# Two channels per filter matmul, product planes instead of finished sums, and a new order of all queues, in a state-space convolution kernel

## The chip, the cores and the metric

The kernel runs on one core of a Trainium2 chip. A core has five instruction queues that run side by side: TensorE (PE, matmuls), VectorE (DVE), ScalarE (ACT), GpSimd (POOL) and SyncE (SP, which issues DMAs here). The metric is the device time of one execution in microseconds; lower is better. The time before is the median of three runs, 216.46 us (214.34 to 217.51).

## The reference

The input u (2048 positions, 512 channels) is normalized; the normalized xn goes two ways. One is a long convolution per channel, whose filter K is built from 128 complex modes; the other is a small gated network on the single position with the largest router score. The result is `x + s * silu(b)`.

```python
P = jnp.exp(logdA[:, :, None] * l[None, None, :])
K = jnp.einsum("dn,dnl,dn->dl", Cc, P, dB).real
...
Yf = Uf * Kf[None, :, :, :]
y = ...irfft2(Yf...)[:, :, 0, :L]
y = y.transpose(0, 2, 1) + u * Dskip
...
g = _silu(_B_ref(xn, B_w_r, B_w_gate, B_w_up, B_w_down))
return x + s * g
```

The positions l are cast to bf16 first, so only 640 different positions occur: K needs 640 values per channel.

## The kernel before

**Filter values.** A filter position is split into a row (32 of them: multiples of 64, some with 1, 2 or 3 added) and a step (26 of them). For each channel, `GG` holds the 128 modes' values at the 32 rows (real and imaginary) and `QQ` those at the 26 steps. One matmul per channel and part (modes are the 128 partitions, 32 rows the weights, 26 steps the moving columns) adds real and imaginary part in PSUM and gives the channel's 32 x 26 filter values. Channels are worked in four quarters of 128: (0,0), (0,1), (1,0), (1,1); the first figure is the half.

**Rows.** `kgen_g` (L1007) starts each quarter from one row (`WW`) and doubles: rows times a complex multiplier `MB[k]` give further rows. `cmul` (L982) does such a product on VectorE in four instructions: two products into scratch `TT` (`TT<-GG,MB`), then two sums or differences from scratch (`GG<-TT`). Seven of them give 1, 2, 4, 4, 8, 4 and 8 rows.

**Steps.** `exps` (L928) and `sines` (L972) make the magnitudes `E` and the phases in `QQ` on ScalarE, 16 instructions of 512 elements each, both halves at once; `turn` (L995) rotates the start row; `kgen_q` (L1020) joins them on VectorE and gets nine more steps by one complex product (`TT<-QQ,MB`, `QQ<-TT`). The chain between them (`SL`, `MB`) squares the multipliers up.

**From filter to spectrum.** `kgen_mm` (L1033) runs the 256 matmuls of a quarter into two PSUM banks and copies them out as `KE`; `kgen_kx` (L1049) moves values to the order of the index table (24 selection matmuls per quarter with 0/1 matrices, copies `KS`, then `KX`). `ROWS` (L318) and `_kpoints` are that index table; the inline table `c_fd` (tile `FD`) is built from it. `spec` (L1125) multiplies `KX` with `FD` (8 groups of 20 matmuls per quarter), copies each group out as `KF` (a ring of seven), and multiplies it into the input's spectrum `UU`. `inv_a` transforms back (copies `C`), `fin` (L1157) ends the inverse, multiplies with the gate `G` and stores.

**The input's way.** Statistics (`ST`, `LST`), normalized `XN`, moved to `XZN` by DMA, two transform stages (`AU`, `UST`), out to DRAM (`scr_u`) and back as `UU`. The router transposes `XN` through `XT`; the network's weights stream through the ring `WRING`.

**Order.** The order of each queue is written out as a list of operation numbers (`ORDER`, L373); an operation waits by semaphore for those that it depends on, also for earlier ones of its own engine. Copies out of PSUM and some small steps can stand in ScalarE's or VectorE's list; the list decides which engine does them. Buffers share memory: `XR` and `G0` lie over `GG`, `UU0` over `XN`, `UU1` over the first half of `QQ`, `F2U` and one `UST` over its second half, `FD` over `AU` and `WRING`. A function asked for by `activation` that lies in another table than the last one costs an `ACT_TABLE_LOAD`.

Of the kernel before, what the change touches and what calls it, by code (L numbers as in the profile page):

```python
# [7 lines left out]
ACT = mybir.ActivationFunctionType  # L8
# [309 lines left out]
ROWS = [64 * r for r in range(16)] + [64 * r + 1 for r in range(4)] + [64 * r + 2 for r in range(8)] + [64 * r + 3 for r in range(4)]  # L318
# [3 lines left out]
def _kpoints():  # L322


    seq = [[], []]
    for par in range(2):
        for jp in range(8):
            seq[par] += [b + 4 * STEPS[2 * jp + par] for b in ROWS]
        for jp in range(4):
            seq[par] += [1024 + b + 8 * (2 * jp + par) for b in ROWS[:16]]  # L330
    return seq[0][:256] + seq[1][:256] + seq[0][256:] + seq[1][256:]


def tables():
# [29 lines left out]
    for q in range(2):  # L364
# [6 lines left out]

ORDER = dict(
    sync="""  # L373
        9-10 12 11 1 6 3 18 7 4 207 211 13 209 205 17 14-15 203 16 145 92 94 93 90 95 91 96-97 146 141 137 140 139 144 138 143 142 150 149 152 151
        147-148 303-304 213 215 217 219 221 309 223 225 427 314 229 231 227 233 319 241 324 243 428 245 247 249 329 545-547 334 251 253 255 257 259
        429 339 261 344 430 548 550 549 644 646-647 268 648-649 645 748 747 746 744 743 745 788 787 785 789 786 790 828 827 832 830 829 831 847
        849-850 855 857-858 848 866 863 874 872 865 864 856 871 873 884 881 883 882 900 898 897 890 916 908 905 907 925-926 906""",
    scalar="""
        5 0 2 8 19-20 35 34 33 28 25-26 23-24 21-22 29 32 30 44 361 360 362 356 358 86-87 89 359 348 354 159 353 355 350 352 347 357 131 133 135 46
        48 363 50 365-367 406 415 364 375 177 399 409 374 398 272 379 274 380 372 381 419 280 407 282 284 386 391 387 288 417 290 393 392 425 294  # L380
        400 296 298 401 300 302 390 412-414 410 420 408 416 421 306 308 311 313 411 418 517 460 316 349 346 351 345 264 321 323 328 326 239 333 331
        616 471 478 476 336 338 480 484 341 343 486 552 531 558 528 564 561 570 533 567 537 535 573 541 539 543 576-577 579-580 654 583 582 651
        585-586 660 657 666 663 672 627 669 630 634 632 679 636 678 676 675 684 681 753 750 759 765 762 729 726 771 731 768 735 775 774 778 833 836
        834-835 804 807 844 810 813 852 783 860 816-817 819 868 823 822 826 878 894 886 910 899 902 891 914 913 920 889 892 915 924 923""",
    vector="""
        202 54 53 62 61 51 57 59 65 56 52 64 104 58 60 66 55 105 63 100 67 103 68 79 154 69 111 70 108 71 101 72 99 73 109 74 107 75 102 76 98 77
        113 78 106 80 112 81 110 88 114 82 115 84 116 85 117 126 83 118 31 119 36 120 37 121 38 122 39 123 27 124 40 125 156 127 42 128 41 132 129
        134 136 130 162 165 168 171 369 174 371 368 370 179 376-377 180 402 181 378 373 276 183 278 383 185 382 423 186 385 187 388 188 286 190 389
        384 394 192 422 193 292 194 395 195 426 424 397 488 197 431 198 461 433 432 396 435 434 518 437 436 403 439 438 441 440 201 442-444 449 445
        447 446 448 451 450 453 452 457 455 454 462 318 456 464 458-459 519 463 520 466 465 265 618 467-468 489-490 266 237 491-492 617 493-494  # L390
        235-236 495-496 238 521 497-498 474 500 499 240 717 501-502 506 504 587 503 620 505 619 508 507 510 509 514 511-512 482 513 716 516 515 487
        523 522 715 524-525 588-589 719 591 590 718 592-593 553 595 594 555 597 596 556 598 559 263 599 267 605 600-601 562 565 603 571 602 568 604
        574 607 606 609 608 613 610-611 269 612 544 614-615 686 622 621 655 623-624 688 687 652 689-690 661 692 691 667 694 693 664 696 695 673 698
        697 658 699-700 704 701-702 670 703 705-708 640 710 709 638 711-712 642 714 713 643 720-721 754 722-723 751 756 760 757 766 685 682 763 733
        772 739 769 737 741-742 777 792-793 795-796 798 838 799 801 840 802 842 839 841 780 805 808 845 781 811 814 853 784 846 854 861 820 862
        869-870 825 879-880 895-896 887 911 888 912 903-904 921-922""",
    gpsimd="""
        404-405 199 270""",
    tensor="""
# [5 lines left out]
        867 821 824 875-877 893 885 909 901 917-919""",  # L405
# [7 lines left out]
def build(nc, A_u, A_A_re, A_A_im, A_B_re, A_B_im, A_C_re, A_C_im, A_log_dt, A_Dskip,  # L413
# [10 lines left out]
    for k in range(4):  # L424
        tri[k, k:] = 1.0
        mk[k, k] = 1.0

    perm = np.zeros((128, 128))
    for p in range(128):
        g_ = 2 * (p // 16 % 2) + p // 64  # L430
        perm[p, 64 * (p // 32 % 2) + 32 * (p // 8 % 2) + 8 * (p % 8 // 2) + 2 * g_ + p % 2] = 1.0
    sel = np.zeros((128, 64))
    for gp in range(4):
        for k in range(16):
            sel[32 * gp + k, 16 * gp + k] = 1.0
    cb_list = [("PRM", perm), ("SEL", sel), ("F1", T["F1"]), ("FA1", T["FA1"]), ("FA2", T["FA2"]), ("IDB", np.eye(128)), ("E127", e127), ("TRI", tri)]
# [30 lines left out]
    with g.ctx:  # L467
# [6 lines left out]
        UPD = g.buf("UPD", o, [512], BF16)  # L474
        GX = g.buf("GX", o + 1024, [64], BF16)
        K2R = g.buf("K2R", o + 2048, [512], BF16)
        X4 = g.buf("X4", o + 3072, [512], BF16)
        DSK0 = g.buf("DSK0", o + 4096, [256], BF16)
        o += 4096 + 512
# [24 lines left out]
        RH = RT + 9 * KB  # L504
        assert RH + 13 * KB + 256 <= 229344 - SBASE, RH + 13 * KB + 256 - 229344 + SBASE

# [39 lines left out]
        KF = [g.buf(f"KF{i}", RH + 1024 * i if i < 4 else RD + 2560 if i == 4 else RH + 10752 + 1024 * (i - 5), [4, 128], BF16) for i in range(7)]  # L546
# [10 lines left out]
        XT = [g.buf(f"XT{i}", RT + 2048 * i, [2, 4, 128], BF16) for i in range(3)]  # L557
        TB = [g.buf(f"TB{i}", RT + 2048 * i, [1024], BF16) for i in range(4)]
        KE = g.buf("KE", RH + 4096, [8, 8, 26], BF16)
        KS = g.buf("KS", RH + 7424, [4, 320], BF16)  # L560
        DSK = [DSK0, g.buf("DSK1", RH + 9984, [256], BF16)]
        WR4 = g.buf("WR4", RH + 10496, [128], BF16)
        WRC = g.buf("WRC", RH + 12800, [4], BF16)
# [141 lines left out]
        for h, p0 in ((0, 32), (0, 96), (1, 32), (1, 96)):  # L705
            load(DSK[h](DSK[h].a.reshape(2, 2, 64), p0, 1), _dma_rows(A_Dskip, 128 * h, [[64, 2], [256, 2], [1, 64]]), 512)
# [68 lines left out]
        for i in range(4):  # L775
            store(sb(X4, i, 1, 0, [[64, 8], [1, 64]]), XN(XN.a[:, :, i].reshape(8, 64), 0, 1), 1024, w=[X4(None, i, 1)])

# [194 lines left out]
        def sines():  # L972
            memset(PO, qboth(0, 0), 1.0)
            memset(PO, qboth(1, 0), 0.0)
            for k in [8] + list(range(1, 8)):
                act(qboth(0, k), TH(), ACT.Sin, scale=float(4 * k), bias=pi2, table="silu", tokr=["set"])
                act(qboth(1, k), TH(), ACT.Sin, scale=float(4 * k), table="silu", tokr=["set"])

        def scratch(n, w):
            return TT.a[0:4 * n * w].reshape(2, 2, n, w)  # L980

        def cmul(dst_r, dst_i, src, mr, mi, n, w, conj):  # L982

            t = scratch(n, w)
            tt(DV, TT(t[0]), src, MB(bc(mr, (2, n, w))), ALU.mult)
# [47 lines left out]
        def kgen_mm(h, s):  # L1033
            q = Q[h]
            for u in range(4 * s, 4 * s + 4):
# [10 lines left out]
                if u % 2:  # L1046
                    evac(KE(KE.a[u - 1:u + 1].reshape(-1)), bank(bank.a[0:416]))

# [218 lines left out]
```

## Time and profile before

| | |
|---|---|
| median of 3 runs | 216.46 us |
| the profiled execution | 217.09 us |
| its span, first to last instruction | 215.3 us |
| mean granted TensorE clock | 0.937 |
| DMA moved | 38.85 MB |

Busy shares are averages over stages with different limits: normalization and router, then the filter's modes with the input's transform beside them, then four rounds of matmuls, spectrum and inverse, then the output. Lines of a view name the tile written and the tiles read (`GG<-TT`), the shape of one instruction, the count, the busy time in us and the mean in ns, and after the second bar the idle time just before them with what ended it. L585 is the helper for all two-input vector operations, L613 and L614 are one copy helper on ScalarE and on VectorE, L580 is the activation helper, and L650 all matmuls, so groups are told apart by their tiles.

### The profile page before, as it was taken

The page shows a single profiled execution, that of the slowest core. Times are in us where ns is not written, and L with a number is a line of the kernel's source. Part 1 is how long each engine was busy: PE and PEld are TensorE (multiplying, and loading weights), DVE is VectorE, ACT ScalarE, POOL GpSimd, SP SyncE. Part 2 cuts the span into 40 slices and gives each one's busy share as a digit, 9 for nine tenths or more (in the row PEclk, how much of TensorE's full clock was granted, in tenths as well). Part 3 has the DMA queues.
Part 4 walks back from the last instruction along what each step waited for, and adds up shares of the span by engine and source line. Part 5 has one row for each costly group of instructions (what it writes and reads, how often), then busy time and mean ns, then how long its engine had stood idle before and what let it go on. Part 6 is the DMA issues. An engine that isn't in the chain of part 4 may idle for free.

```text
span 215.3 us, 6844 instructions
## 1 busy us (share of the span) xinstructions
PE 155.0 (72%) x2979; PEld 130.0 (60%) x2979; DVE 186.1 (86%) x385; ACT 145.2 (67%) x230; POOL 4.6 (2%) x8
## 2 busy tenths in 40 slices
PE   0043977998487159859886897698799799977560
PEld 0033866876354037636785786698699789876430
DVE  1999999899999889999997699679999457989692
ACT  2579999999999456653133589534971249989961
POOL 2000000001100000000000020000000000000000
PEclk9999999999999999985998899799999889999955
DMA  6940959600678969999599802920059299971457
GB/s 223 376 172 32 160 116 223 259 3 0 203 288 212 364 207 299 329 279 334 141 365 237 209 7 54 292 53 6 0 157 228 47 377 268 182 122 33 100 111 149
DMA packets 37181, 38.85 MB, mean 180 GB/s; under 512 B 10816, under 2 KB 29728, under 8 KB 36640
## 3 DMA queue, kind: packets, MB, share of 16 engines
q1 hardware_dynamic: 34704, 37.53, 62.4%
q10 hardware_dynamic: 2384, 0.90, 1.7%
q8 instruction: 23, 0.38, 0.8%
q14 instruction: 6, 0.05, 0.1%
q0 software_dynamic: 64, 0.00, 0.0%
HBM read 27.92 MB, written 8.39 MB: 169 GB/s over the span
## 4 chain that ended last, share of the span: by engine, by line
ACT 37%; PE 33%; DVE 14%; DMA 9%; issue 4%; SPq 2%; ACTq 0%
PE PB L650 33%; ACT C L621 12%; DMA scr_u<-UST 5%; DVE ST L743 4%; ACT AU L613 4%; ACT G L580 3%; DVE TT L585 3%; ACT UST L613 3%; ACT QQ L580 3%; ACT E L580 2%; SPq L667 2%; DMA XZN<-XN 2%; ACT XN L766 2%; ACT TB L580 2%; DMA X<-in_A_u_dram 2%
## 5 line engine op out<-in xcount | busy, mean ns | idle before, releaser
L650 PE MATMUL PB<-KX,FD 128*128 128x128 bf16 x640 | 45.2, 235 | 6.1 <-ACT KF L613 4.2
L650 PEld LDWEIGHTS PB<-KX,FD 128*128 128x128 bf16 x640 | 41.4, 107 | 8.8 <-ACT KF L613 4.7
L585 DVE TENSOR_TENSOR TT<-GG,MB 128x1024 bf16<-128x1024 bf16 (+3 forms) x56 | 39.3, 741 | 0.1
L613 ACT ACTIVATE KF<-PB 128x512 bf16<-128x512 f32 x26 | 15.4, 599 | 29.0 <-PE PB L650 22.7
L621 ACT ACTIVATE C<-PB 64x512 bf16<-64x512 f32 x48 | 28.3, 590 | 3.7 <-PE PB L650 2.8
L585 DVE TENSOR_TENSOR UU<-UU,KF 128x1024 bf16<-128x1024 bf16 x32 | 21.5, 685 | 6.7 <-ACT KF L613 6.6
L650 PE MATMUL PB<-QQ,GG 128*32 128x26 bf16 x1024 | 21.4, 233 | 3.5 <-issue 2.6
L650 PEld LDWEIGHTS PB<-QQ,GG 128*32 128x32 bf16 x1024 | 19.9, 173 | 5.6 <-issue 3.6
L650 PE MATMUL PB<-AU,F2U 64*128 64x256 bf16 x128 | 14.6, 380 | 11.9 <-ACT UST L613 8.2
L585 DVE TENSOR_TENSOR GG<-TT 128x512 bf16<-128x512 bf16 (+3 forms) x56 | 22.9, 445 | 0.1
L613 ACT ACTIVATE UST<-PB 128x1024 bf16<-128x1024 f32 x15 | 14.9, 1027 | 10.0 <-DMA scr_u<-UST 6.4
L650 PE MATMUL PB<-CB,UU 128*128 128x128 bf16 x256 | 19.2, 229 | 3.1 <-ACT C L621 2.0
L650 PEld LDWEIGHTS PB<-CB,UU 128*128 128x128 bf16 x256 | 17.3, 150 | 4.7 <-ACT C L621 2.9
L650 PE MATMUL PB<-CB,XZN 32*128 32x64 bf16 x256 | 16.2, 343 | 2.3 <-DMA XZN<-XN 0.8
L650 PEld LDWEIGHTS PB<-AU,F2U 64*128 64x128 bf16 x128 | 7.2, 123 | 15.6 <-ACT UST L613 9.6
L650 PEld LDWEIGHTS PB<-CB,XZN 32*128 32x128 bf16 x256 | 13.4, 200 | 4.8 <-ACT AU L613 2.2
L743 DVE BATCH_NORM_STATS2 ST<-X 128x6 f32<-128x512 bf16 x16 | 10.3, 676 | 3.8 <-DMA X<-in_A_u_dram 3.8
L650 PE MATMUL PB<-CB,XN 128*64 128x128 bf16 x128 | 8.3, 314 | 6.4 <-DVE XN L767 5.2
L613 ACT ACTIVATE AU<-PB 128x1024 bf16<-128x1024 f32 x12 | 12.1, 1028 | 0.1
L585 DVE TENSOR_TENSOR QQ<-QQ,E 128x896 bf16<-128x896 bf16 (+1 forms) x12 | 10.3, 865 | 1.9 <-ACT E L580 1.0
L626 DVE CAST C<-PB 64x512 bf16<-64x512 f32 x16 | 11.0, 689 | 0.8 <-PE PB L650 0.5
L650 PEld LDWEIGHTS PB<-CB,XN 128*64 128x64 bf16 x128 | 6.6, 169 | 7.4 <-DVE XN L767 5.5
(122 smaller groups left out, 241.1 us busy)
## 6 DMA issues: line engine op xcount, KB each, us to landing
FD<-c_fd SPq DMA_DIRECT2D x4, 1280.0 KB, 6.0
scr_u<-UST SPq DMA_DIRECT2D x8, 512.0 KB, 7.2
UU<-scr_u SPq DMA_DIRECT2D x8, 512.0 KB, 7.9
UU<-scr_u SPq DMA_DIRECT2D x16, 256.0 KB, 8.3
X<-in_A_u_dram SPq DMA_DIRECT2D x4, 512.0 KB, 6.2
XZN<-XN SPq DMA_DIRECT2D x16, 128.0 KB, 3.8
scr_g<-XN SPq DMA_DIRECT2D x4, 512.0 KB, 6.4
G<-scr_g SPq DMA_DIRECT2D x1, 2048.0 KB, 8.9
```

What stands on the lines that cost most here:

```text
L580: g.op(AC, lambda e: e.activation(out=out.ap, in_=in_.ap, func=func, **kw), w=[out], r=r, cost=cost(AC, out, 0.834) - (43 if in_.buf.space ...
L585: g.op(eng, lambda e: e.tensor_tensor(out=out.ap, in0=a.ap, in1=b.ap, op=op), w=[out], r=[a, b], cost=cost(eng, out, rate))
L613: g.op(AC, lambda e: e.activation(out=out.ap, in_=in_.ap, func=ACT.Copy), w=[out], r=[in_], cost=cost(AC, out, 0.834) - 43, alt=(DV, lambd ...
L621: ins = e.activation(out=o_.ap, in_=i_.ap, func=ACT.Copy)
L626: ins = e.tensor_copy(out=o_.ap, in_=i_.ap)
L650: ins = e.matmul(o_.ap, lhsT=l_.ap, rhs=r_.ap, start=st, stop=sp, **kw)
L667: fn = lambda e: e.dma_start(dst, src)
L743: g.op(DV, lambda e, b=b: e.bn_stats(ST6(ST6.a[b]).ap, X0(X0.a[b]).ap), w=[ST6(ST6.a[b])], r=[X0(X0.a[b])], cost=620)
L766: flex(ov, [iv, mv_, nv, rv], lambda e, ov=ov, iv=iv, nv=nv, rv=rv: e.activation(out=ov.ap, in_=iv.ap, func=ACT.Identity, bias=nv.ap, scal ...
```

## The change

- **Rows.** Doubling stops at 12 rows (1 + 1 + 2 + 4 + 4, planes 20 to 31 of `GG`). The last two row products (12 rows times `MB[6]`, 8 rows times `MB[3]`) fill planes 0 to 19. In the second half (`PROD` false) they are finished by sums as before, in one step each. In the first half (`PROD` true) the four product planes stay: re times re and im times re in `GG`, im times minus im (`NM`) and re times im in a new tile `GP`; the matmuls add them up, four per channel pair where the second half has two.
- **Matmuls.** Two channels lie in one matmul: 64 weight columns (40 for `GP`), 52 moving columns; two column groups of 64 instead of four of 32. 1024 matmuls become 512 + 256. `KE` is copied out four times a quarter instead of twice, and the selection matmuls go from 24 of full width to 48 of half width a quarter.
- **Complex products** write the first product into the destination and add in place.
- **Halves.** `exps`, `sines` and `turn` run per half: 32 + 32 instructions of 256 elements instead of 16 + 16 of 512. `DSK1` is loaded later.
- **Memory.** `TT` halves, `GP` and `NM` are new, `KF` is a ring of five, `XT` lies over the second half of `QQ`, `X4` goes into `K2R`.
- **Index table and order.** `ROWS` is re-ordered to follow the planes (and with it `c_fd` and the selection matrices); all five lists of `ORDER` are new, with other choices of engine for the copies.

```diff
-ROWS = [64 * r for r in range(16)] + [64 * r + 1 for r in range(4)] + [64 * r + 2 for r in range(8)] + [64 * r + 3 for r in range(4)]
+ROWS = [64 * r for r in range(8, 16)] + [64 * r + 2 for r in range(8)] + [64 * r + 3 for r in range(4)] + [64 * r for r in range(8)] + [64 * r + 1 for r in range(4)]
...
+PROD = [True, True, False, False]
...
-        GG = g.buf("GG", RF, [2, 32, 256], BF16)
+        GG = [g.buf(f"GG{i}", RF + 16 * KB * i, [2, 32, 128], BF16) for i in range(2)]
...
-        TT = g.buf("TT", RT, [4608], BF16)
+        TT = g.buf("TT", RT, [2304], BF16)
+        GP = g.buf("GP", RT + 4608, [2, 20, 128], BF16)
...
-            for i in range(16):
-                o_ = 4 * i if i < 9 else -4 * (i - 8)
-                act(E(E.a[:, i]), AR(AR.a.reshape(2, 256)), ACT.Exp, scale=float(32 + o_), table="exp")
+            for h in range(2):
+                g.stage = f"exps{h}"
+                for i in range(16):
+                    o_ = 4 * i if i < 9 else -4 * (i - 8)
+                    act(E(E.a[h, i]), AR(AR.a[256 * h:256 * h + 256]), ACT.Exp, scale=float(32 + o_), table="exp")
...
+        def cmul(buf, dst, src, mr, mi, n, w, conj):
+
+            t = TT.a[0:2 * n * w].reshape(2, n, w)
+            tt(DV, buf(dst), src, MB(bc(mr, (2, n, w))), ALU.mult)
+            tt(DV, TT(t), src, MB(bc(mi, (2, n, w))), ALU.mult)
             a, b = (ALU.add, ALU.subtract) if conj else (ALU.subtract, ALU.add)
+            tt(DV, buf(dst[0]), buf(dst[0]), TT(t[1]), a)
+            tt(DV, buf(dst[1]), buf(dst[1]), TT(t[0]), b)
...
-            todo = [(0, 1, 1, 0), (0, 2, 2, 1), (0, 4, 4, 2), (0, 16, 4, 5), (0, 20, 8, 6), (16, 28, 4, 6), (0, 8, 8, 3)]
...
+            for lo, m, n, k in [(0, 1, 1, 0), (0, 2, 2, 1), (0, 4, 4, 2), (0, 8, 4, 5)]:
+                cmul(G, gs[:, m:m + n], G(gs[:, lo:lo + n]), *mb(k), n, 128, True)
+            g.stage = f"p{h}{s}"
+            for i, (k, n, d) in enumerate(((6, 12, 8), (3, 8, 0))):
+                mr, mi = mb(k)
+                src = G(gs[:, 0:n])
+                if PROD[2 * h + s]:
+                    tt(DV, G(G.a[:, d:d + n]), src, MB(bc(mr, (2, n, 128))), ALU.mult)
+                    tt(DV, GP(GP.a[0, d:d + n]), G(gs[0, 0:n]), NM(bc(NM.a[i, cs], (n, 128))), ALU.mult)
+                    tt(DV, GP(GP.a[1, d:d + n]), G(gs[1, 0:n]), MB(bc(mi, (n, 128))), ALU.mult)
+                else:
+                    t = GP.a.reshape(-1)[0:2 * n * 128].reshape(2, n, 128)
+                    tt(DV, G(G.a[:, d:d + n]), src, MB(bc(mr, (2, n, 128))), ALU.mult)
+                    tt(DV, GP(t), src, MB(bc(mi, (2, n, 128))), ALU.mult)
+                    tt(DV, G(G.a[0, d:d + n]), G(G.a[0, d:d + n]), GP(t[1]), ALU.add)
+                    tt(DV, G(G.a[1, d:d + n]), G(G.a[1, d:d + n]), GP(t[0]), ALU.subtract)
...
+            for u in range(4):
+                bank = PB[u % 2]
...
+                for mi in range(8):
+                    for buf, pl, n_, ri in ((G, 0, 32, 0), (GP, 1, 20, 0), (GP, 0, 20, 1), (G, 1, 32, 1))[::1 if four else 3]:
+                        for g2 in range(2):
+                            m = 32 * g2 + 8 * u + mi
+                            lst.append((bank(bank.a[52 * mi:52 * mi + 52].reshape(2, 26), 64 * g2, 2 * n_), two(buf, pl, n_, m), q(qv[ri, :, :, m].transpose(1, 0)), buf is G and ri == 0, buf is G and ri == 1, (0, 64 * g2)))
+                mm(lst, 23 if four else 28)
+                evac(KE(KE.a[8 * u:8 * u + 8].reshape(-1)), bank(bank.a[0:416]))
...
-                kf = KF[kp % 7]
+                kf = KF[kp % 5]
```

The new lists mix the statistics of both halves of the positions (before, those of the first half were finished first). On ScalarE the exponentials and sines of the first half come before the `UST` copies and those of the second half among them, in alternating runs. On SP one load of `UU` for quarter (0,1) stands ahead of the last `FD` piece and of the second half of `UU` for (0,0). On VectorE the products of spectrum and filter come after most of quarter (1,0)'s filter work, and on PE the matmuls of (1,0) come next to the start of (0,1)'s spectrum.

More of the change, by code (lines that the diff above doesn't have):

```diff
@@ L329, in _kpoints @@
         for jp in range(4):
-            seq[par] += [1024 + b + 8 * (2 * jp + par) for b in ROWS[:16]]
+            seq[par] += [1024 + b + 8 * (2 * jp + par) for b in range(0, 1024, 64)]
     return seq[0][:256] + seq[1][:256] + seq[0][256:] + seq[1][256:]
@@ L430, in build @@
         g_ = 2 * (p // 16 % 2) + p // 64
[L431 to L436, printed above, removed]
+        perm[p, 64 * (p // 32 % 2) + 32 * (p // 8 % 2) + 8 * g_ + 2 * (p % 8 // 2) + p % 2] = 1.0
+    sel, idh = np.zeros((128, 2, 32)), np.zeros((128, 2, 64))
+    for half in range(2):
+        for g2 in range(2):
+            for r in range(32):
+                idh[64 * g2 + 2 * r + half, half, 32 * g2 + r] = 1.0
+            for k in range(16):
+                sel[64 * g2 + 2 * SPOT[64 * k] + half, half, 16 * g2 + k] = 1.0
+    sel, idh = sel.reshape(128, 64), idh.reshape(128, 128)
+    cb_list = [("PRM", perm), ("SEL", sel), ("IDH", idh), ("F1", T["F1"]), ("FA1", T["FA1"]), ("FA2", T["FA2"]), ("IDB", np.eye(128)), ("E127", e127), ("TRI", tri)]
     p_ = np.arange(128)
@@ L473, in build @@
         o += cfa.shape[1] * 4
[L474 to L479, printed above, removed]
+        UPD = g.buf("UPD", o - cfa.shape[1] * 4, [512], BF16)
+        GX = g.buf("GX", o, [64], BF16)
+        K2R = g.buf("K2R", o + 128, [512], BF16)
+        DSK0 = g.buf("DSK0", o + 1152, [256], BF16)
+        NM = g.buf("NM", o + 1664, [2, 256], BF16)
+        o += 2688
         SML = g.buf("SML", o, [64], F32)
@@ L972, in sines @@
         def sines():
[L973 to L985, printed above, removed]
-            tt(DV, TT(t[1]), src, MB(bc(mi, (2, n, w))), ALU.mult)
+            for h in range(2):
+                g.stage = f"sines{h}"
+                qh = lambda ri, i: QQ(QQ.a[h, i, ri])
+                th = TH(TH.a[256 * h:256 * h + 256])
+                memset(PO, qh(0, 0), 1.0)
+                memset(PO, qh(1, 0), 0.0)
+                for k in [8] + list(range(1, 8)):
+                    act(qh(0, k), th, ACT.Sin, scale=float(4 * k), bias=pi2, table="silu", tokr=["set"])
+                    act(qh(1, k), th, ACT.Sin, scale=float(4 * k), table="silu", tokr=["set"])
+        def cmul(buf, dst, src, mr, mi, n, w, conj):
+            t = TT.a[0:2 * n * w].reshape(2, n, w)
+            tt(DV, buf(dst), src, MB(bc(mr, (2, n, w))), ALU.mult)
+            tt(DV, TT(t), src, MB(bc(mi, (2, n, w))), ALU.mult)
             a, b = (ALU.add, ALU.subtract) if conj else (ALU.subtract, ALU.add)
-            tt(DV, dst_r, TT(t[0, 0]), TT(t[1, 1]), a)
-            tt(DV, dst_i, TT(t[0, 1]), TT(t[1, 0]), b)
+            tt(DV, buf(dst[0]), buf(dst[0]), TT(t[1]), a)
+            tt(DV, buf(dst[1]), buf(dst[1]), TT(t[0]), b)
         def neg(out, in_):
@@ L1063, in kgen_kx @@
                     for par in range(2):
[L1064 to L1066 removed]
+                        for half in range(2):
+                            c0 = w_ * (jp - j0) + w_ // 2 * half
+                            lst.append((bank(bank.a[c0:c0 + w_ // 2], pp + nb * par, nb), KE(KE.a[:, half, col(jp, par)]), CB(mv_[w_ // 2 * half:w_ // 2 * half + w_ // 2]), True, True, (0, pp + nb * par)))
+                mm(lst, 25)
                 n_ = (j1 - j0) * w_ // 4
@@ L1099, in build @@
         sines()
-        g.stage = "turn"
-        turn()
         def kgen(h, s):
+            if s == 0:
+                turn(h)
+                if h:
+                    g.stage = "ldo"
+                    load_d(1)
+                g.stage = f"nm{h}"
+                for i, k in enumerate((6, 3)):
+                    neg(NM(NM.a[i]), MB(MB.a[k, 1, 256 * h:256 * h + 256]))
             g.stage = f"g{h}{s}"
-            kgen_g(h, 128 * s, 128 * s + 128)
+            kgen_g(h, s)
             g.stage = f"q{h}{s}"
```

150 lines of the change are left out of this document (71 added, 79 removed), and 10 rows, old and new, of the table tensor.

## The prediction

> **What bounds the kernel now.** I read the page first (busy shares, slices, the chain's shares), then the sums by window, then groups by form, then the timeline.
>
> ```profile
> span 215.3 us, 6844 instructions
> ...
> PE 155.0 (72%) x2979; PEld 130.0 (60%) x2979; DVE 186.1 (86%) x385; ACT 145.2 (67%) x230; POOL 4.6 (2%) x8
> ...
> DVE  1999999899999889999997699679999457989692
> ACT  2579999999999456653133589534971249989961
> ...
> ACT 37%; PE 33%; DVE 14%; DMA 9%; issue 4%; SPq 2%; ACTq 0%
> ```
>
> The chain gives ScalarE the largest share, but a chain picks one of several ways where queues run neck and neck. The slices say more: VectorE is full from the second slice to about the 21st, ScalarE only to the 13th.
>
> ```profile
> 17.00:60.00 43.00, 32.77 (x512) 27.26 (x514) 41.33 (x105) 42.76 (x68) 1.79 (x1) 1.00 0.52 132
> 60.00:104.00 44.00, 31.29 (x545) 20.69 (x540) 41.76 (x75) 26.58 (x36) 0.00 (x0) 0.92 0.94 289
> ...
> 163.00:178.00 15.00, 13.15 (x379) 12.11 (x372) 8.97 (x15) 4.34 (x9) 0.00 (x0) 0.89 0.67 214
> 178.00:215.00 37.00, 25.56 (x411) 21.41 (x409) 28.77 (x51) 29.28 (x38) 0.00 (x0) 0.86 0.69 136
> ```
>
> Columns: window, length, busy of PE, its weight loads, VectorE, ScalarE, GpSimd, then clock, DMA share, GB/s. From 17 to 60 us VectorE and ScalarE are both full; from 60 to 104 VectorE has 41.8 of 44 and ScalarE 17.4 idle; after 163 VectorE idles 6.0 + 8.2 us. So the filter generation on VectorE sets the pace until its last complex product, and what follows is a tail shared by all engines.
>
> ```profile
> 161.23 1.41 DVE L585 TENSOR_TENSOR QQ<-TT 128x1152 bf16<-128x1152 bf16 x2
> ```
>
> That product ends at 162.6; the tail is 52.7 us. This execution took 217.1 us, 1.8 more than its span; the median of the runs is 216.5, so 0.6 below it.
>
> **VectorE.**
>
> ```profile
> L585 DVE TENSOR_TENSOR UU<-UU,KF 128x1024 bf16<-128x1024 bf16 x32 | 21.5, 685 | 6.7 <-ACT KF L613 6.6
> L585 DVE TENSOR_TENSOR TT<-GG,MB 128x2048 bf16<-128x2048 bf16 x16 | 19.4, 1220 | 0.0
> L585 DVE TENSOR_TENSOR TT<-GG,MB 128x1024 bf16<-128x1024 bf16 x24 | 15.5, 682 | 0.1
> ...
> L585 DVE TENSOR_TENSOR GG<-TT 128x1024 bf16<-128x1024 bf16 x16 | 10.3, 686 | 0.1
> L585 DVE TENSOR_TENSOR GG<-TT 128x512 bf16<-128x512 bf16 x24 | 9.3, 418 | 0.0
> L614 DVE CAST XT<-PB 128x1024 bf16<-128x1024 f32 x6 | 7.2, 1221 | 0.5 <-PE PB L650 0.4
> ...
> L614 DVE CAST KF<-PB 128x512 bf16<-128x512 f32 x6 | 4.1, 678 | 0.0
> ...
> L767 DVE TENSOR_SCALAR XN<-X,LST 128x512 bf16<-128x512 bf16 x10 | 3.7, 409 | 0.0
> ...
> L614 DVE CAST KX<-PB 128x256 bf16<-128x256 f32 x5 | 2.1, 421 | 1.2 <-PE PB L650 1.2
> ...
> L595 DVE COPY GG<-WW 128x256 bf16<-128x256 bf16 x4 | 0.8, 212 | 0.2 <-PE PB L650 0.2
> ```
>
> ```profile
> 69.69 1.29 DVE L585 TENSOR_TENSOR GG<-TT 128x1024 bf16<-128x1024 bf16 x2
> ```
>
> Two sums of mean 0.686 take 1.29 together, so in a full queue an instruction costs its mean less 0.08: 1.14 for 2048 elements, 0.60 for 1024, 0.34 for 512; from the slope 1.67 for 3072 and 0.87 for 1536. Before, the last three row products of a quarter (8, 4 and 8 rows) cost 3.48 + 1.88 + 3.48 = 8.84. In the first half, product planes cost 1.67 + 2 x 0.87 + 1.14 + 2 x 0.60 = 5.75, with no sums: 3.1 less, twice. In the second half the 12- and 8-row products cost 8.56: 0.28 less, twice. Together -6.7. Sums in place are no dearer (UU<-UU is in place, at 0.685).
>
> The two vector lists, counted instruction by instruction up to the last sum of the last quarter, differ in three more ways. Five of the seventeen spectrum products that stood ahead of it now stand behind: 5 x 0.60 = -3.0. Copies that went to ScalarE: two XT and one UST (3.4), three KX (1.0), a KF, a KE (1.1), two XN (0.7): -6.2. Taken on: one AU (1.14), one WW (0.6), four NM negations at the 256-wide copy's price (0.14 each; the two of the second half are read by nobody), two PAR (0.4), two negations (0.7), the halved turn (0.2): +3.6. Sum 12.3. With the same idle as before, the last quarter is ready at 150.3 instead of 162.6. But the list behind it grows by 6.6 (12.3 less the 5.7 that leave VectorE altogether), against 14.2 us of tail idle. It hides fully or not at all at the ends; I take half, since half of that idle is scattered in waits of under 2 us: +3.3.
>
> **ScalarE.**
>
> ```profile
> L613 ACT ACTIVATE UST<-PB 128x1024 bf16<-128x1024 f32 x15 | 14.9, 1027 | 10.0 <-DMA scr_u<-UST 6.4 <-PE PB L650 3.6
> ...
> L580 ACT ACTIVATE QQ<-TH 128x512 bf16<-128x512 f32 x16 | 9.1, 633 | 0.0
> L580 ACT ACTIVATE E<-AR 128x512 bf16<-128x512 f32 x16 | 8.8, 614 | 0.0
> ...
> L580 ACT ACTIVATE TB<-PB 128x1024 bf16<-128x1024 f32 x6 | 6.0, 1024 | 0.9 <-DVE TB L585 0.7 <-PE PB L650 0.2
> L580 ACT ACT_TABLE_LOAD x4 | 5.1, 1283 | 2.9 <-issue 2.8
> ...
> L613 ACT ACTIVATE KE<-PB 128x416 bf16<-128x416 f32 x7 | 3.6, 518 | 9.7 <-PE PB L650 9.7
> ...
> L580 ACT ACTIVATE TB<-PB 128x512 bf16<-128x512 f32 x4 | 2.4, 599 | 1.7 <-PE PB L650 1.7
> ```
>
> ```profile
> 68.96 1.28 ACT L580 ACT_TABLE_LOAD   x1
> 70.25 2.19 ACT L580 ACTIVATE E<-AR 128x512 bf16<-128x512 f32 x4
> ...
> 98.31 0.28 ACT L613 ACTIVATE KX<-PB 128x128 bf16<-128x128 f32 x1
> ```
>
> The slope of TB (425 ns for 512 elements) makes a 256-wide exponential or sine 0.40 to 0.42, and 0.31 in a row (four E in 2.19 overlap by 0.09). Splitting 16 + 16 into 32 + 32 adds 1.6 + 1.6. KE copies go from 8 to 16 at 0.44. Up to the last KX copy of the first quarter (98.3 to 98.6) the list holds 5.1 us more. And it switches tables: exponentials, sines, exponentials, sines and so on, ten loads instead of four, nine of them ahead of that copy (one more if the table taken for a sine lacks Silu; no row shows that): 5 x 1.28 = 6.4, then one ahead of the four G activations of the tail, which I put on the path: +1.3. So 11.5 more work ahead of that copy, under 17.4 idle. I take it as hidden; without cover it would be 11.5.
>
> The Trainium skill ("ScalarE: Activation LUTs", "What ACT_TABLE_LOAD costs" and "Table sets: the hidden batching unit") counts 1.38 us of drain on top of 1.28, and says to finish one set before the next, which the new order does not. By it six more loads would be 16.0 us, not 7.7, and an estimate of the end 217.7; the trace agrees on 1.28, and its next exponential starts 0.01 after the load, so it shows no drain.
>
> **PE.**
>
> ```profile
> 140.48 1.33 PE L650 MATMUL PB<-QQ,GG 128*32 128x26 bf16 x64
> ...
> 142.96 2.75 PE L650 MATMUL PB<-QQ,GG 128*32 128x26 bf16 x128
> ...
> 150.65 0.45 PE L650 MATMUL PB<-CB,KE 128*32 128x64 bf16 x8
> ...
> 187.65 0.64 PE L650 MATMUL PB<-C,FB 128*64 128x128 bf16 x16
> ...
> 201.23 0.41 PE L650 MATMUL PB<-C,FB 128*64 128x128 bf16 x8
> ```
>
> 64 more matmuls of 26 columns take 1.42: 22 ns each, 22.7 for 1024. The new shape (64 or 40 weight columns, 52 moving) lies between that and C,FB (64 weights, 128 moving: 0.23 for 8, 29 ns): 768 take 16.9 to 22.3. The selection matmuls double from 96 to 192 at half width, 0 to 3.5 us by the KE row's 36 ns above a 0.16 start. Net -5.8 to +3.1; I take 0, as the gain and the loss both stand in gaps of PE.
>
> **Queues.**
>
> ```profile
> UU<-scr_u SPq DMA_DIRECT2D x16, 256.0 KB, 8.3
> ```
>
> On SP one load for quarter (0,1) now stands ahead of the last FD piece and the second half of UU for (0,0). It waits for the last kernel matmul of (0,1); who waits behind it are spectrum groups 6 and 7 and the products of groups 4 to 7. VectorE reaches those after some 113.5 us of work instead of 107, so I cost it 0; with a late matmul up to 8.3.
>
> **Sum:** 217.1 - 12.3 + 3.3 + 1.3 = 209.4; 0.6 below for the median, 209 rounded.
>
> **Rivals.** *ScalarE sets the pace (slower).*
>
> ```profile
> 17.15 2.22 ACT L766 ACTIVATE XN<-X,LST 128x512 bf16<-128x512 bf16 x3 [0.18 <-DVE LST L603]
> ```
>
> The first normalization stood behind 12.6 us of vector work and now behind 15.6, as statistics of both halves are mixed: ScalarE starts it 3.0 later. If all its idle of 60 to 104 comes again (each UST copy follows a matmul pair and a store; that row alone has 10.0 of waits), it is late by 11.5 + 3.0 = 14.5. Exponentials and sines of the second half stand among those copies, and VectorE waits for them one for one, less about 2 us of slack: 209.4 + 12.5 = 221.9, and the more so the dearer a switch is. It decides from the point where the last exponential comes after 100 us; after 112 the change loses. For: nothing pre-computes that half. Against: the 17.4, and the restart 0.01 after a load. Chance 0.18. The table rule of the Trainium skill's ScalarE page speaks for this rival. *The saving is waited for.* Only the 10.0 of UST waits return: late by 14.5 - 7.4 = 7.1, 216.5; a tail that hides nothing (212.7) plus SP's queue ends there too. The busy share would fall without the time. Chance 0.20. *All of it counts.* The extra 6.6 hide, PE gains half its bound: 217.1 - 12.3 + 1.3 - 2.9 = 203.2; for it, no engine is full after 163. Chance 0.12. The forecast has 0.50.
>
> **Numbers.** A measurement of this kernel tells about 2% from no change: 212.1 and 220.8. Of the forecast's own 203 to 214, 0.42 is faster and 0.08 within; the waited-for case gives 0.04 and 0.16. Faster 0.42 + 0.04 + 0.12 = 0.58, within 0.24, slower 0.18. The range runs from 201 to 221, into the cases at both ends.
>
> **What would show it.** Matmuls with GG: 768 in all. No sums with GP in the first half; VectorE near 180 busy. Ten or eleven table loads, each near 1.28, the next instruction at once behind. The last quarter's product ending near 150; if it ends after 158, the forecast is wrong. VectorE idle behind E or QQ from ScalarE between 75 and 105 says the slower rival; idle behind KF or DMA, the waited-for one.

## The result and the profile after

Four runs of the changed kernel took 238.79 us in the median (237.13 to 240.81); the kernel before took 216.26 beside them. The ratio is 1.1025, with a 95% interval of 1.0909 to 1.1141: slower by about a tenth, where 209 was forecast, and outside the range of 201 to 221. Here and below a ratio leaves out runs that took over 1.5% longer than the fastest of the same kernel, here the one of 240.81. The profiled execution took 237.13 us, 20.0 more than that of before.

The page of the changed kernel, its span, busy shares, slices and chain:

```profile
span 235.3 us, 6571 instructions
...
PE 184.1 (78%) x2819; PEld 157.7 (67%) x2819; DVE 179.7 (76%) x375; ACT 159.5 (68%) x276; POOL 6.7 (3%) x10
...
PE   0035767898295489979999969999989999999751
...
DVE  1999999999499984489960594949294388999982
...
PE 42%; ACT 25%; DVE 20%; DMA 9%; issue 2%; ACTq 1%; DVEq 0%
PE PB L660 42%; ACT C L631 5%; DVE ST L756 4%; DMA FD<-c_fd 4%; DMA GX<-scr_g,SMI 3%; ACT G L590 3%; DVE QQ L595 3%; DVE GG L595 3%; ACT SL L590 3%; ACT XN L779 2%; ACT AU L623 2%; DMA X<-in_A_u_dram 2%; ACT XT L623 2%; DVE XR L595 1%; ACT TB L590 1%
```

VectorE works 6.4 us less than before, as the change says, but its idle time in the span grows from 29.2 to 55.6 us: its slices, full before from the second to the 21st, have holes from the 11th on. TensorE is nearly full from the 16th slice to the 37th and carries 42% of the chain, 33% before. The sums by window (columns as in the prediction) say the same, with PE's 37.00 of 37 us in the last line:

```profile
60.00:104.00 44.00, 33.62 (x465) 24.98 (x465) 32.17 (x58) 34.58 (x60) 0.00 (x0) 0.69 0.79 253
...
178.00:215.00 37.00, 37.00 (x625) 35.30 (x624) 27.60 (x48) 28.03 (x38) 0.00 (x0) 0.91 0.64 176
```

The groups by form name the work. Of the kernel matmuls there are 768, as announced, but each is long, and ScalarE waits 36.4 us for them before its copies `KE`, where it waited 9.7 before:

```profile
L660 PE MATMUL PB<-QQ,GG 128*64 128x52 bf16 x512 | 46.7, 314 | 2.1 <-DVE GP L595 2.1
...
L660 PE MATMUL PB<-QQ,GP 128*40 128x52 bf16 x256 | 26.0, 294 | 0.0
L590 ACT ACT_TABLE_LOAD x11 | 14.1, 1283 | 3.1 <-issue 2.9
...
L590 ACT ACTIVATE E<-AR 128x256 bf16<-128x256 f32 x32 | 11.5, 408 | 0.1
...
L623 ACT ACTIVATE KE<-PB 128x416 bf16<-128x416 f32 x16 | 8.2, 515 | 36.4 <-PE PB L660 36.4
```

The means of 314 and 294 ns overlap each other, so the price is read from the timeline, where one line is one stretch of equal instructions; here the last quarter:

```profile
177.04 8.92 PE L660 MATMUL PB<-QQ,GG 128*64 128x52 bf16 x128
```

From the first start to the last the 128 matmuls take 8.61 us: 68 ns each, where the last quarter's 256 took 19 and 30 ns each before (one half of them and the other; 17 to 30 in all quarters). In the first half, where 64 and 40 weight columns alternate, it is 57 ns. Added up over all stretches of PE that hold only kernel matmuls, each from its first to its last start, that is 46.1 us against 21.7 before: 24.4 more. I call this sum the matmul time below; it holds the stops inside a stretch too.

### The profile page after: what moved, and what is told of

It reads as the page before. It is cut to its first block, busy times and chain, and to the rows that moved or that the text cites. A ratio compares the mean times of both kernels' runs of the same rounds, so it can differ in the third digit from the quotient of the medians.

```text
span 235.3 us, 6571 instructions
## 1 busy us (share of the span) xinstructions
PE 184.1 (78%) x2819; PEld 157.7 (67%) x2819; DVE 179.7 (76%) x375; ACT 159.5 (68%) x276; POOL 6.7 (3%) x10
## 4 chain that ended last, share of the span: by engine, by line
PE 42%; ACT 25%; DVE 20%; DMA 9%; issue 2%; ACTq 1%; DVEq 0%
PE PB L660 42%; ACT C L631 5%; DVE ST L756 4%; DMA FD<-c_fd 4%; DMA GX<-scr_g,SMI 3%; ACT G L590 3%; DVE QQ L595 3%; DVE GG L595 3%; ACT SL L590 3%; ACT XN L779 2%; ACT AU L623 2%; DMA X<-in_A_u_dram 2%; ACT XT L623 2%; DVE XR L595 1%; ACT TB L590 1%
## 5 line engine op out<-in xcount | busy, mean ns | idle before, releaser
L660 PE MATMUL PB<-QQ,GG 128*64 128x52 bf16 x512 | 46.7, 314 | 2.1 <-DVE GP L595 2.1
L660 PE MATMUL PB<-KX,FD 128*128 128x128 bf16 x640 | 42.0, 226 | 3.2 <-DMA FD<-c_fd 2.3
L660 PEld LDWEIGHTS PB<-QQ,GG 128*64 128x64 bf16 x512 | 41.7, 237 | 3.7 <-DVE GP L595 2.5
L660 PEld LDWEIGHTS PB<-KX,FD 128*128 128x128 bf16 x640 | 38.2, 101 | 5.8 <-issue 3.0
L623 ACT ACTIVATE KE<-PB 128x416 bf16<-128x416 f32 x16 | 8.2, 515 | 36.4 <-PE PB L660 36.4
L660 PE MATMUL PB<-QQ,GP 128*40 128x52 bf16 x256 | 26.0, 294 | 0.0
L660 PEld LDWEIGHTS PB<-CB,UU 128*128 128x128 bf16 x256 | 19.0, 153 | 1.8 <-ACT C L631 0.6
L595 DVE TENSOR_TENSOR GG<-GG,MB 128x1024 bf16<-128x1024 bf16 (+4 forms) x24 | 19.8, 836 | 0.0
L660 PEld LDWEIGHTS PB<-QQ,GP 128*40 128x40 bf16 x256 | 17.9, 191 | 0.0
L636 DVE CAST C<-PB 64x512 bf16<-64x512 f32 x18 | 12.3, 684 | 5.2 <-PE PB L660 5.0
L590 ACT ACTIVATE E<-AR 128x256 bf16<-128x256 f32 x32 | 11.5, 408 | 0.1
```

The source lines that it names most:

```text
L590: g.op(AC, lambda e: e.activation(out=out.ap, in_=in_.ap, func=func, **kw), w=[out], r=r, cost=cost(AC, out, 0.834) - (43 if in_.buf.space ...
L595: g.op(eng, lambda e: e.tensor_tensor(out=out.ap, in0=a.ap, in1=b.ap, op=op), w=[out], r=[a, b], cost=cost(eng, out, rate))
L623: g.op(AC, lambda e: e.activation(out=out.ap, in_=in_.ap, func=ACT.Copy), w=[out], r=[in_], cost=cost(AC, out, 0.834) - 43, alt=(DV, lambd ...
L636: ins = e.tensor_copy(out=o_.ap, in_=i_.ap)
L660: ins = e.matmul(o_.ap, lhsT=l_.ap, rhs=r_.ap, start=st, stop=sp, **kw)
```

## The experiments

**Pairs and planes undone.** The first three runs take back the two halves of the matmul change, alone and together, and leave the order, the halves, the table loads and the copies' engines.

```diff
-                        for g2 in range(2):
-                            m = 32 * g2 + 8 * u + mi
-                            lst.append((bank(bank.a[52 * mi:52 * mi + 52].reshape(2, 26), 64 * g2, 2 * n_), two(buf, pl, n_, m), q(qv[ri, :, :, m].transpose(1, 0)), buf is G and ri == 0, buf is G and ri == 1, (0, 64 * g2)))
+                        for gp in range(4):
+                            c = 64 * (gp // 2) + 32 * (gp % 2) + 8 * u + mi
+                            lst.append((bank(bank.a[26 * mi:26 * mi + 26], 32 * gp, n_), buf(buf.a[pl, 0:n_, c]), q(q.a[ri, :, 128 * s + c]), buf is G and ri == 0, buf is G and ri == 1, (0, 32 * gp)))
```

> The changed kernel with one channel per kernel matmul again: 32 weight columns (20 for the product planes) and 26 moving columns in four column groups, copies of 208 elements, 24 selection matmuls of full width a quarter; everything else of the change stays. Theory A (weights and moving columns follow one another inside a column group, and two groups do half of what four do): a round of the four groups takes 72 ns as before, so 18 to 22 ns a matmul; 2 x 512 + 2 x 256 matmuls take about 30 us instead of the 47 that 512 + 256 took, and as these lie on the path the time falls by about 17, to 222 (218 to 226). Rival B (ScalarE with its eleven table loads sets the pace): the matmuls get cheaper all the same, but the time stays above 230.

Measured: 229.5 us (ratio to before 1.0657, 1.0542 to 1.0772), 9.3 less than the changed kernel and not 17. Where instructions come without a stop a matmul takes 18 ns in the second half, as expected, and 15 in the first, where 32 and 20 weight columns alternate. But often they don't come: the timeline of PE has stops for which no semaphore is the reason.

```profile
85.87 0.27 PE L656 MATMUL PB<-QQ,GG 128*32 128x26 bf16 x3
89.54 0.27 PE L656 MATMUL PB<-QQ,GG 128*32 128x26 bf16 x5 [3.40 <-issue]
...
93.55 0.24 PE L656 MATMUL PB<-QQ,GP 128*20 128x26 bf16 x3 [1.50 <-issue]
```

The bracket holds the idle time before a line and what ended it; "issue" means nothing that the profile shows. With these stops the matmul time is 42.6 us, hardly less than with pairs. Rival B expected a time above 230, and 229.5 is no verdict between the two; the next runs give it.

```diff
-PROD = [True, True, False, False]
+PROD = [False, False, False, False]
```

> The changed kernel with the pairs kept, but in the first half too the last two row products are finished by sums on VectorE, and no product planes are added up by matmuls: 512 kernel matmuls instead of 768. Theory A: a quarter of the first half falls from 14.7 us on PE to the 8.9 of the second half, 11.6 us less in all, and VectorE takes about 6 more; time 229 (226 to 233). Rival C (the product planes were no part of the loss, since their matmuls hide beside VectorE): the time rises by the added VectorE work, to 240 or more.

> Both undone: one channel per matmul in four column groups, and sums on VectorE in the first half; queue order, halves, table loads, copies moved between engines and memory plan of the change stay. Theory A: PE has the 23 us of the kernel before instead of 47; the time comes to 216 to 221, and what is left against the kernel before is what order and table loads cost. Rival B (ScalarE sets the pace): above 230.

Measured: 236.33 us with the pairs kept and 228.38 with both undone. Both are above what theory A said, and the waits of VectorE show why (here of the second; 7.1 in the first): by the new place of one product VectorE stood 7.0 us behind ScalarE's copy of a multiplier, a stop of these two kernels' own making.

```profile
DVE GG L589 <- ACT MB L943: 7.0, 1, 7.0
```

Both were run again with that product later in VectorE's list.

> As the run with pairs and with sums in the first half, with the same mend of VectorE's list. Theory A: the 7 us come off 236, to 229 (227 to 232), since the matmuls take 34 us instead of 46 and lie on the path. Rival D: 235 to 237 again.

> As the run with both undone (one channel per matmul, sums on VectorE in the first half), but the product with the third multiplier stands later in VectorE's list, so that VectorE doesn't wait 7.0 us for ScalarE's copy of that multiplier. Theory A: the 7 us come off, 221 (219 to 224); the 4 to 5 above the kernel before are what the order and the table loads cost. Rival D (the wait was covered by later idle time): 227 to 229 as in that run, and then the queue order and table loads cost 12 by themselves.

Measured: 228.88 us for the pairs with sums (ratio 1.0535, 1.045 to 1.062) and 220.45 with both undone (1.0149, 1.0075 to 1.0222), as theory A said. So the planes cost 10 us in the changed kernel, pairs and planes together 18 of its 22.5, and what stays with the new order and its eleven table loads is 3 us above before. Rival B falls with this run, as all eleven table loads are in it.

**Where the elements lie.** A pair of matmuls in two column groups should not be slower than the row of `C` and `FB`, which has as many weight columns and more than twice the moving ones at 29 ns. One thing differs that no view's column shows: there the 64 weights lie side by side, and the moving columns come in two runs of 64; here every 64th element (128 bytes apart) is a weight, and the moving columns that follow one another are two steps of one channel, 512 elements (1024 bytes) apart. Three runs change that spacing and nothing else in the instructions. These three, and three of the later ones, read other elements than the filter needs and so compute other filter values; they serve for the price alone. (The text of the second speaks of moving columns 64 elements apart; that is the distance of the two channels, not that of two reads in a row.)

```diff
-            two = lambda buf, pl, n_, m: buf(buf.a[pl, 0:n_].reshape(2 * n_, 64)[:, m])
+            two = lambda buf, pl, n_, m: buf(buf.a[pl, 0:n_].reshape(-1)[2 * n_ * m:2 * n_ * m + 2 * n_])
...
-q(qv[ri, :, :, m].transpose(1, 0))
+q(q.a[ri, m % 52 // 2, 128 * s + 52 * (m % 2):128 * s + 52 * (m % 2) + 52].reshape(2, 26))
```

> The changed kernel with each matmul reading 64 (or 40) weights that lie side by side in a plane instead of every 64th element; the filter values are other ones by this, the count and shape of all instructions stay. Theory A1 (the serial pass of 64 + 52 columns costs what it does wherever the elements lie): a pair of matmuls still takes 137 ns, 69 ns a matmul in the second half. Theory A2 (weights that lie 128 bytes apart are read slowly): the part from the start of a weight load to its matmul falls from 84 ns to under 60, and a matmul of the second half takes 40 to 55 ns.

> The changed kernel with the 52 moving columns of each kernel matmul side by side in one plane instead of 64 elements apart; the weights stay 64 elements apart; the filter values are other ones by this, the count and shape of all instructions stay. After side-by-side weights alone brought a matmul of the second half from 68 to 44.5 ns: theory A2a (only the weights' spacing is slow) says 68 ns stay and the time is 236 to 241; theory A2b (moving columns that lie apart are slow as well) says the part from a matmul's start to the next weight load, 52 ns, halves, a matmul takes 50 to 58 ns, and the time falls to 228 to 233.

> The changed kernel with both weights and moving columns side by side; the filter values are other ones by this, the count and shape of all instructions stay. Theory A2b: the matmul comes to what the row of C and FB led the prediction to, 22 to 32 ns, 768 of them to 17 to 25 us instead of 46, and the time to 215 to 220. Theory A2a: 44.5 ns as with side-by-side weights alone, 34 us, and the time to 223 to 226.

The last quarter in the timelines of the three, in this order, and of the third also a stretch of quarter (1,0) without a stop:

```profile
167.19 5.96 PE L660 MATMUL PB<-QQ,GG 128*64 128x52 bf16 x128
```

```profile
167.79 7.26 PE L660 MATMUL PB<-QQ,GG 128*64 128x52 bf16 x128
```

```profile
133.73 1.20 PE L660 MATMUL PB<-QQ,GG 128*64 128x52 bf16 x64
...
154.44 1.99 PE L660 MATMUL PB<-QQ,GG 128*64 128x52 bf16 x96
...
156.64 0.69 PE L660 MATMUL PB<-QQ,GG 128*64 128x52 bf16 x32 [0.21 <-ACT KE L623]
```

Measured: 224.78 us with the weights side by side (one run), 227.23 with the moving columns side by side (median of four), 210.51 with both (ratio to before 0.9708, 0.9622 to 0.9793). Matmuls of the last quarter take 45, 55 and 21 ns. In stretches of the third kernel without a stop it is 16 ns, and 14 in the first half, where 64 and 40 weight columns alternate. The matmul time is 34.0, 36.8 and 18.3 us. Theory A1, by which 64 + 52 columns cost 68 ns wherever they lie, falls; A2b holds for the price, while the last two times came below its ranges (228 to 233 and 215 to 220). The instructions, their shapes and their order are those of the changed kernel in all three: the spacing alone is worth 28 us.

**What else could set the time.** Two runs with the cheap matmuls try the table loads and the planes.

```diff
-E x2, UST x2, E x4, sine x1, UST x2, sine x6, E x1, KE, E x2, sine x1
+sine x8, E x2, UST x2, E x4, UST x2, E x1, KE, E x2
```

(This diff gives the stretch of ScalarE's list in words; that of the other run is the line of `PROD` above.)

> As the run with weights and moving columns side by side, but with all sines of the second half on ScalarE ahead of its exponentials: three of the eleven table loads go, 3.9 us. The rival of the prediction (ScalarE sets the pace): the time falls by 3 to 4, to 207. The forecast (hidden under ScalarE's idle time): within 1 of that run's 210.5.

> As the run with weights and moving columns side by side, but with sums on VectorE in the first half instead of product planes: what the planes bring where the matmuls are cheap. VectorE works 5.7 longer, PE has 256 matmuls less (at 14 to 24 ns: 4 to 6 us). The prediction's step says 210.5 + 5.7, less what hides: 214 to 216; a rival (PE gives it back) 210 to 212.

The table loads of the first of them:

```profile
L588 ACT ACT_TABLE_LOAD x8 | 10.3, 1283 | 2.9 <-issue 2.7
```

Measured: 210.85 us with three loads less, against 210.51: nothing, as the forecast said of hidden loads. And 210.78 with sums in place of planes, as the rival said and not the prediction's step: here the planes bring nothing. PE's matmul time falls from 18.3 to 14.0, VectorE's busy time rises by 5.7, and the two come out even.

**A version that computes the filter with close operands.** The rows are stored in blocks of 8 channels, so that the weights of a pair (channels c and c+4) stand 4 elements apart; VectorE's operands then come in runs of 8 side by side, in two instructions for each product into the rows, and the first steps of quarter (0,1) stand a little later in its list.

```diff
+        for b in GG:
+            b.a = b.a.reshape(2, 16, 32, 8).transpose(0, 2, 1, 3)
...
-            two = lambda buf, pl, n_, m: buf(buf.a[pl, 0:n_].reshape(2 * n_, 64)[:, m])
+            two = lambda buf, pl, n_, m: buf(buf.a[pl, 0:n_, m // 4, m % 4::4].reshape(2 * n_))
...
-q(qv[ri, :, :, m].transpose(1, 0))
+q(q.a[ri, :, 128 * s + 8 * (m // 4) + m % 4:128 * s + 8 * (m // 4) + 8:4])
```

> The changed kernel computing the same filter as before, but with the rows stored so that the 64 weight columns of a pair stand 4 elements (8 bytes) apart instead of 64 (128 bytes), and the two channels of a step stand 4 elements apart too: channels are taken in blocks of 8, each block holding its 32 rows one after another, and the pair is (c, c+4). Each product into rows is two vector instructions (real, imaginary) instead of one, 40 more in all, which adds about 3 us to VectorE. The Trainium skill (SBUF - State Buffer, the note on cachelines) says that reads run at full bandwidth with at least two hits in a line of 16 bytes. Theory A3 (a penalty for each element that lies far from the one before): a kernel matmul takes 14 to 27 ns as with side-by-side reads, and the time is 211 to 217. Rival E (any reading that isn't side by side is slow): 45 to 68 ns and 226 to 241. Rival F (the vector instructions with runs of 8 elements lose their speed): VectorE above 200 us busy and the time above 228.

Measured: 213.66 us, ratio to before 0.9892 (0.9781 to 1.0004), and 25 us below the changed kernel. Timeline and groups:

```profile
157.78 4.10 PE L661 MATMUL PB<-QQ,GG 128*64 128x52 bf16 x128
```

```profile
L1000 DVE TENSOR_TENSOR GG<-GG,MB 128x1536 bf16<-128x1536 bf16 x8 | 7.3, 947 | 0.0
```

A matmul takes 30 ns here and 25 in the first half; the matmul time is 22.1. VectorE's instructions lose nothing by the blocks: 947 ns for 1536 elements, 952 in the changed kernel (a product into `GP`); there are 44 more of them, and its busy time is 3.0 us longer. Theory A3 holds, though the 30 ns lie a little above its 27, and rivals E and F fall. Against the kernel before the interval just touches 1, so that it is the faster one is likely and not settled.

Which operand keeps the last 10 ns, and whether place or order of reading counts, is asked by two kernels, with one run each:

> The version with weights 8 bytes apart, with the 52 moving columns of each kernel matmul side by side in one plane; the filter values are other ones by this. If weights 8 bytes apart read as fast as side-by-side ones, a matmul takes 14 to 16 ns where instructions keep up, as with both side by side; if they cost the 10 ns that are left, 25 ns stay.

> The version with weights 8 bytes apart, with the same 52 moving elements of a pair read in another order: all 26 steps of one channel, then those of the other, so that no two elements that follow one another stand near each other; all else and the result stay. If the order counts (two reads in a row near each other), a matmul goes from 25 to 30 up to 40 to 55 ns; if only the weights' spacing or the set of addresses counts, it stays at 25 to 30.

```profile
157.71 4.05 PE L661 MATMUL PB<-QQ,GG 128*64 128x52 bf16 x128
```

```profile
169.44 6.16 PE L661 MATMUL PB<-QQ,GG 128*64 128x52 bf16 x128
```

The first (213.53 us) changes nothing: beside these weights, moving columns that come in pairs 8 bytes apart cost no more than side-by-side ones, and what is left is the weights. The second (227.4 us) reads the same addresses in the other order and takes 46 ns in all quarters: it is the order that counts. The Trainium skill ("SBUF — State Buffer", "Specifications (TRN2)") gives SBUF lines of 16 bytes and asks for two hits in a line for full speed; the moving columns agree (25 to 30 against 46 ns), the weights do not: two in a line still cost 25 to 30 ns where side by side 14 to 16 were seen.

> The version with weights 8 bytes apart, without product planes (sums on VectorE in the first half) and with all sines of the second half ahead of its exponentials (8 table loads). At 25 to 30 ns a matmul the 256 matmuls that go take 6 to 7 us off PE, and VectorE works 5.7 longer; with side-by-side reads that exchange came out even at 14 to 24 ns. If the matmuls lie on the path, 211 to 213; if VectorE's added work counts in full, 215 to 217; the table loads count for nothing, as measured.

```diff
-PROD = [True, True, False, False]
+PROD = [False, False, False, False]
```

Measured: 215.58 us (ratio 1.01, 1.0048 to 1.0152; the medians of all runs are 215.58 and 216.11 before). That is the case in which VectorE's added work counts. With matmuls of 25 to 30 ns the planes are worth about 2 us, from runs on two occasions (213.66 with planes), and this is no better version.

## Why the prediction was wrong

| kernel | profiled run, us | matmul time, us | difference |
|---|---|---|---|
| changed | 237.1 | 46.1 | 191.0 |
| weights side by side | 224.8 | 34.0 | 190.8 |
| moving columns side by side | 226.5 | 36.8 | 189.7 |
| both side by side | 210.7 | 18.3 | 192.4 |
| 8 bytes apart | 213.6 | 22.1 | 191.5 |
| the same, other order of reading | 227.4 | 35.1 | 192.3 |
| before | 217.1 | 21.7 | 195.4 |
| pairs, sums in place of planes, product later | 228.4 | 34.3 | 194.1 |
| no pairs, sums, product later | 220.0 | 24.7 | 195.3 |
| both side by side, sums | 210.7 | 14.0 | 196.7 |
| no pairs, planes kept | 227.9 | 42.6 | 185.3 |

**The step that failed** is the price on PE: "The new shape (64 or 40 weight columns, 52 moving) lies between that and C,FB [...]: 768 take 16.9 to 22.3." The terms were sized by the columns of one matmul. The measured matmul time is 46.1, so PE's net was not between -5.8 and +3.1 but +24 by these matmuls alone. Neither end of the range was a row of the same kind:

- The upper end was a row whose operands lie side by side. With side-by-side reads the new matmuls take 18.3 us, within the bounds: the shape was priced rightly, its operands were not.
- The lower end, 22 ns, had operands that lie far apart too (weights 512 bytes, moving columns 1024), but it is a quarter of a round. In the trace of the kernel before four weight loads start within 10 ns of one another and then four matmuls within 11 ns, one for each column group, and the next round begins some 65 to 70 ns later. In the changed kernel two loads and two matmuls start so, and the next round begins about 137 ns later. A matmul with twice the columns takes twice as long in its group (1.2 ns for each of 58 or 116 columns), and two groups work where four did. So a pair saves nothing while its operands are read from afar, and each channel costs double. This is worked out from the starts; no run changes the number of groups alone.

The net was also taken as 0 because gain and loss stand in gaps of PE; the table shows that the matmuls count in full. In its first six rows, where the matmul time goes from 18 to 46 us, the whole time follows one for one within 3 us. The last row falls out of this: some of the stops that its matmul time holds seem to have stood beside other waits, which was not tried.

**VectorE.** The busy time (179.7, forecast near 180), the absent sums and the count of matmuls came as said. The last complex product of the rows ends at 176.0 in the changed kernel, past the 158 that was named as the sign of a wrong forecast. With side-by-side reads it ends at 153.4, forecast 150.3. The line of the changed kernel, then that of side-by-side reads:

```profile
174.73 1.29 DVE L595 TENSOR_TENSOR GG<-GG,GP 128x1024 bf16<-128x1024 bf16 x2
```

```profile
152.13 1.28 DVE L595 TENSOR_TENSOR GG<-GG,GP 128x1024 bf16<-128x1024 bf16 x2
```

That is 9.2 of the 12.3 us. Its tail is 55.4 us of that span of 208.8, where the sum had 57.3 (52.7 + 3.3 + 1.3). So for matmuls as cheap as it assumed the forecast of 209 holds within 2 us, but partly by luck, as terms cancel: in the table's last column the planes are worth 3 to 4 us outside the matmuls, not 6.2, and the copies moved and spectrum products deferred, 5.6 in the sum, bring nothing that the table shows (195.3 against 195.4). The 3 us by which that kernel is slower than before are in its matmul time (24.7 against 21.7), by longer stops of PE (5.3 us against 2.0); outside it the new order and the table loads cost nothing that the table shows.

**ScalarE.** Eleven loads of 1.283 us (ten or eleven forecast), and 408 ns for an exponential of half width (0.40 to 0.42): right, and hidden as far as the run with three loads less can show. VectorE never waited for `E` or for `QQ`'s sines between 75 and 105 us, so the slower rival is not what happened; its 221.9 was nearer only by luck. What VectorE waits for is PE, which no rival had: 30.6 us in all, against 9.9 before and 12.5 with side-by-side reads.

```profile
DVE UPD L605 <- PE PB L660: 10.1, 1, 10.1
...
DVE SMB L605 <- PE PB L660: 7.0, 2, 3.8
DVE C L636 <- PE PB L660: 5.0, 3, 3.8
...
DVE UU L595 <- DMA UU<-scr_u: 4.4, 2, 3.2
DVE UU L595 <- ACT KF L623: 3.9, 3, 3.0
```

**Queues.** SP's moved load was costed at 0, with up to 8.3 behind a late matmul. The wait of VectorE for `UU` from DRAM is 4.4 us in the changed kernel and 2.2 with cheap matmuls; no run takes it out by itself, so its share in the result stays open.

## What to carry to other kernels

Price a small matmul by how its operands are read and by how many column groups work beside it, not by its columns alone: a row of another matmul bounds it only if both are alike, and the spacing stands in the code, not in the profile's shape. When two items are packed into one matmul, choose as partners two that lie within a few bytes of each other and read them one after the other. If a time falls one for one with the sum of one group's stretches over several variants, that group is on the path, whatever the gaps around it looked like before.

## What the runs showed of the hardware

- **Spacing.** 64 weights and 52 moving columns in two column groups took 68 ns a matmul with weights 128 and moving columns 1024 bytes apart, 45 with weights side by side, 55 with moving columns side by side, and 16 in stretches without a stop with both.
- **Column groups.** With operands far apart, a round of four groups (32 weights, 26 moving columns each) took 65 to 70 ns, and a round of two groups (64 and 52) about 137.
- **Instructions.** With 1536 small matmuls PE stopped for 3.40, 1.50 and 1.51 us in the first quarter and for 3.98 and 4.08 in the second half, with no semaphore to wait for. In the window from 82 to 101 us the instruction queue moved three packets, and each of the first three stops ends 1.3 to 1.5 us after one of them has landed:

```profile
q8 instruction: 3, 0.05, 1.2%
```

  In the traces of all sixteen kernels 19 such stops of over 0.6 us stand before kernel matmuls (two of them in the kernel before), and each ends 1.3 to 1.6 us after a packet of this queue has landed. The six kernels whose matmuls take 44 ns or more, the changed one among them, have none. That these stops are the fetch of instructions is read from this nearness and was not tried by itself. The Trainium skill ("Runtime: NRT & Kernel Launch", "Instruction fetch mechanics") says that instructions come in blocks of 16 KiB (256 instructions) and that crossing a block is mostly hidden. The size agrees with the three packets' 0.05 MB; if the stops are this fetch, the hiding does not hold for matmuls of 15 to 30 ns.
- **Clock.** The granted clock (third column from the right in the windows) does not show in the price of these matmuls. In the first run with pairs and sums it was 0.50 in one stretch of 64 of them and 1.00 in another, and both stretches took 68 ns a matmul:

```profile
92.90:97.30 4.40, 4.36 (x64) 4.36 (x64) 4.19 (x6) 1.90 (x4) 0.00 (x0) 0.50 0.00 0
...
144.00:148.40 4.40, 4.40 (x66) 4.36 (x64) 2.26 (x5) 1.11 (x2) 0.00 (x0) 1.00 0.87 247
```
